# First-layer weights moved in three whole transfers behind the first unit's product, and the second chunk's loads released by units 1 and 2

## The chip, the cores and the metric

The kernel runs on one core of one Trainium2 chip. The metric is the device time of one execution in microseconds (us); the time of the kernel before is 248.93 us, the median of three runs that lie between 248.78 and 249.1 us. One more execution was recorded by the hardware profiler, and every row below is from it.

## The reference, cut to what matters

A linear attention with a decaying state is followed by a two-layer feed-forward network with SiLU. The attention runs over batch 4, 8 heads, 768 steps and 48 channels a head; the network has 3072 tokens of 384 values and a hidden width of 2048.

```python
def _attn_ref(r, k, v, w, u):
    state = np.zeros((B, H, D, D), dtype=np.float32)
    for t in range(S):
        kt, vt, rt = (k[:, :, t].copy(), v[:, :, t].copy(), r[:, :, t].copy())
        cur = np.einsum('bhd,bhe->bhde', u[None] * kt, vt)
        y[:, :, t] = np.einsum('bhd,bhde->bhe', rt, state + cur)
        state = w[None, :, :, None] * state + np.einsum('bhd,bhe->bhde', kt, vt)

def _moe_ref(x, w_in, w_out):
    h = x @ w_in
    g = h * (1.0 / (1.0 + np.exp(-h)))
    return g @ w_out
```

All inputs and the output are float32. The attention's output, as 3072 rows of 384, is the network's x.

## The kernel before

The 768 steps are cut into 6 chunks of 128. A **unit** is one chunk of one batch element: 24 units, unit i being chunk i // 4 of batch i % 4. Units 0 to 3 are the first chunk, and from unit 4 on a unit also needs the state that the unit four before it left.

Inputs live in four slots (`rin`, `kin`, `vin`, NIN = 4), so unit 4 loads into the slot of unit 0. `load(i)` (line 63) issues three transfers from SyncE, for r, k and v of a unit. Each brings 192 KB, in pieces of 48 values (192 bytes). Units 0 to 3 are loaded at the start. SyncE's queue is in program order, so a transfer that has to wait holds all that stand behind it.

For each unit there are four steps, spread over four turns of the main loop (line 303), s being the turn:

- `p1(s)` transposes r and k of unit s on TensorE (`tr`, `tk`, line 172), and VectorE scales them out of PSUM (`rT`, `kT`). In the same turn `natural(s)` puts on GpSimd the three products `ku`, `rku_f` and `kc` (lines 148, 150, 151) and casts v on ScalarE (line 146). `bonus(s)` reduces `rku_f` on VectorE and makes `vu` from it on GpSimd (line 160).
- `p2(s - 1)` makes the scores of the unit before (`ae`, `ao`, lines 186 and 188) and masks them (`am`).
- `p3(s - 2)` makes the outputs `y` and the state's update `sps` (lines 208 and 216).
- `p4(s - 3)` transposes the output into `xT` (lines 254, 255), the network's input.

The network's work is cut into pieces that the list `fillers` holds; `fill(2)` puts some of it between the attention's steps. A block of units adds its pieces once its last unit is through `p4`. The first block is units 0 and 1, so its first-layer matmuls (`hps`, line 263) come behind `p1(4)`, `p2(3)`, `p3(2)` and `p4(1)` in TensorE's order. They read `win` (three tiles of 128 x 2048 in float16, one for each 128 of the 384 inputs), and the second layer's (`ops`, line 275) read `wout`.

Both weights are float32 in memory and are cast to float16 by the transfer itself, which GpSimd issues: `win` in twelve transfers of 128 x 512 in turn 1 (line 310), `wout` in four of 128 x 4 x 384 in turn 3 (line 315). GpSimd takes its instructions in order too, so its products for the units stand behind the issues.

The loads of units 4, 5 and 6 are issued in turn 3. The first of them is made to wait, by a dependency written by hand, for `last_pool[3]`, the `vu` of unit 3, which stands behind the issues of `wout` on GpSimd. From turn 4 on `load(s + 3)` follows turn by turn. The four state tiles `st` are cleared by GpSimd in turn 0 (line 321).

Of the kernel before, what the change touches and what calls it, by code (L numbers as in the profile page):

```python
# [11 lines left out]
ALU = mybir.AluOpType  # L12
# [3 lines left out]
def kernel(  # L16
# [11 lines left out]
    nc = tc.nc  # L28

    B, H, S, D = r.shape  # L30
# [8 lines left out]
    NQ = HD // 128  # L39
    NU = B * NCH  # L40
    NIN = 4
    NKC = 3
# [9 lines left out]
    kin = [big.tile([128, H, 64], FP, name=f"kin{i}") for i in range(NIN)]  # L52
    vin = [big.tile([128, H, D], FP, name=f"vin{i}") for i in range(NIN)]
    kc = [big.tile([128, H, 64], F16, name=f"kc{i}") for i in range(NKC)]
    st = [big.tile([PR, NP, PW], FP, name=f"st{b}") for b in range(B)]
    st16 = [big.tile([PR, NP, PW], F16, name=f"stb{b}") for b in range(B)]
    win = [big.tile([128, DFF], F16, name=f"win{q}") for q in range(NQ)]
    wout = big.tile([128, NFT, HD], F16)

    def unit(i):  # L60
        return divmod(i, B)

    def load(i, after=None):
        if i >= NU:
            return
        sc, b = unit(i)
        for t, src in ((rin, r), (kin, k), (vin, v)):
            d = nc.sync.dma_start(out=t[i % NIN][:, :, 0:D],
                                  in_=src[b, :, sc * C:sc * C + C, :]
                                  .rearrange("h t d -> t h d"))  # L70
            if after is not None:
                tc.add_manual_dep(d.ins, after.ins.name,
                                  mybir.DependencyInfo(mybir.DependencyClass.Sync,
                                                       mybir.DependencyReason.DATA),
                                  reason="the weights go first")
                after = None
# [4 lines left out]
    for p0, o in ((0, 0), (64, D)):  # L81
        nc.scalar.dma_start(out=wpT[p0:p0 + D, :],
                            in_=bass.AP(tensor=w.tensor, offset=o, ap=[[1, D], [PW, NP]]))
# [9 lines left out]
    for t in (rin, kin):  # L93
# [7 lines left out]
        out=maskM, in_=maskM, compare_op=ALU.is_ge, fill=0.0,  # L101
# [19 lines left out]
    n = 1  # L121
    while n < C:
        for t, o in ((pw, 1), (iw, 0)):
            nc.vector.tensor_tensor(
                out=t[:, :, o + n:o + 2 * n], in0=t[:, :, o:o + n],
                in1=t[:, :, o + n - 1:o + n].broadcast_to([PR, NP, n]), op=ALU.mult)
# [6 lines left out]
    lamC = cst.tile([128, H, D], FP)  # L133
# [5 lines left out]
    last_pool = {}  # L139

    def natural(i):

        n = i % NIN
        L = live.setdefault(i, {})
        L["v16"] = wrk.tile([128, H, D], F16, name="v16", bufs=4)
        nc.scalar.copy(out=L["v16"], in_=vin[n])
        ku = wrk.tile([128, H, D], FP, name="ku")
        nc.gpsimd.tensor_tensor(out=ku, in0=kin[n][:, :, 0:D], in1=u_bc, op=ALU.mult)  # L148
        L["rku_f"] = wrk.tile([128, H, D], FP, name="rku_f")
        nc.gpsimd.tensor_tensor(out=L["rku_f"], in0=rin[n][:, :, 0:D], in1=ku, op=ALU.mult)  # L150
        nc.gpsimd.tensor_tensor(out=kc[i % NKC][:, :, 0:D], in0=kin[n][:, :, 0:D],  # L151
                                in1=lamC, op=ALU.mult)

    def bonus(i):
        L = live[i]
        rku = wrk.tile([128, H], FP, name="rku")
        nc.vector.tensor_reduce(out=rku, in_=L["rku_f"], axis=mybir.AxisListType.X,  # L157
                                op=ALU.add)
        L["vu"] = wrk.tile([128, H, D], FP, name="vu", bufs=3)
        last_pool[i] = nc.gpsimd.tensor_tensor(  # L160
            out=L["vu"], in0=vin[i % NIN],
            in1=rku.unsqueeze(2).broadcast_to([128, H, D]), op=ALU.mult)

    def p1(i):
        n = i % NIN
        L = live.setdefault(i, {})
        tr = ps.tile([128, NP, C], FP, name="tr", tag="ps", bufs=8)
        tk = ps.tile([128, NP, C], FP, name="tk", tag="ps", bufs=8)
        for t, src in ((tr, rin), (tk, kin)):
            flat = src[n].rearrange("p h d -> p (h d)")  # L170
            for p in range(NP):
                nc.tensor.transpose(t[0:PR, p, :], flat[:, 128 * p:128 * p + PR], ident)  # L172
        L["rT"] = wrk.tile([PR, NP, C], FP, name="rT")
        nc.vector.tensor_tensor(out=L["rT"], in0=tr[0:PR], in1=lamR, op=ALU.mult)  # L174
        L["kT"] = wrk.tile([PR, NP, C], FP, name="kT")
        nc.vector.tensor_tensor(out=L["kT"], in0=tk[0:PR], in1=lamK, op=ALU.mult)  # L176
        if i >= B:
            L["rT16"] = wrk.tile([PR, NP, C], F16, name="rT16", bufs=3)
            nc.scalar.copy(out=L["rT16"], in_=L["rT"])  # L179

    def p2(i):
        L = live[i]
        ae = ps.tile([128, NP, C], FP, name="ae", tag="ps", bufs=8)
        ao = ps.tile([128, NP, C], FP, name="ao", tag="ps", bufs=8)
        for p in range(NP):
            nc.tensor.matmul(ae[:, p, :], L["kT"][0:D, p, :], L["rT"][0:D, p, :],  # L186
                             start=True, stop=True)
            nc.tensor.matmul(ao[:, p, :], L["kT"][64:PR, p, :], L["rT"][64:PR, p, :],  # L188
                             start=True, stop=True)
        L["am"] = []  # L190
        for a in (ae, ao):
            am = wrk.tile([128, NP, C], F16, name="am", bufs=4)
            nc.vector.tensor_tensor(out=am, in0=a,  # L193
                                    in1=maskM.unsqueeze(1).broadcast_to([128, NP, C]),
                                    op=ALU.mult)
            L["am"].append(am)
# [49 lines left out]
    def p4(i):  # L246
        L = live.pop(i)
        bl = block_of[i]
        if bl.xT is None:
            bl.xT = wrk.tile([128, NQ, B, C], F16, name="xT", bufs=3)  # L250
        yT = ps.tile([128, NQ, C], F16, name="yT", tag="ps", bufs=8)
        yf = L["y16"].rearrange("p h d -> p (h d)")
        for q in range(NQ):
            nc.tensor.transpose(yT[:, q, :], yf[:, 128 * q:128 * q + 128], ident16)  # L254
        nc.scalar.copy(out=bl.xT[:, :, bl.units.index(i), :], in_=yT)  # L255
# [28 lines left out]
    def moe(bl):  # L284
        w1 = bl.n / B
        for ft in range(NFT):
            yield w1, lambda ft=ft: l1(bl, ft)
        for j in range(bl.n):
            for part in range(4):
                yield 1.0, lambda j=j, part=part: l2(bl, j, part)  # L290
# [4 lines left out]
    def fill(n):  # L295
        owed[0] = min(owed[0] + n, n + 1.0)
        while fillers and owed[0] > 0:
            w_, f = fillers.pop(0)
            owed[0] -= w_
            f()  # L300


    for s in range(NU + 3):
        if s < NU:
            p1(s)
            natural(s)
        if s == 1:
            for g in range(4):
                for q in range(NQ):
                    nc.gpsimd.dma_start(out=win[q][:, 512 * g:512 * g + 512],  # L310
                                        in_=moe_w_in[128 * q:128 * q + 128,
                                                     512 * g:512 * g + 512])
        if s == 3:
            for g in range(4):
                nc.gpsimd.dma_start(
                    out=wout[:, 4 * g:4 * g + 4, :],
                    in_=moe_w_out[512 * g:512 * g + 512, :]
                    .rearrange("(f p) n -> p f n", p=128))
        if s == 0:
            for b in range(B):  # L320
                nc.gpsimd.memset(st[b], 0.0)
        fill(2)
        if 0 <= s - 1 < NU:
            p2(s - 1)
        fill(2)
        if s < NU:
            bonus(s)
        if s == 3:
            load(4, after=last_pool[3])
            load(5)  # L330
            load(6)
        elif s > 3:
            load(s + 3)
        if 0 <= s - 2 < NU:
            p3(s - 2)
        fill(2)
        if 0 <= s - 3 < NU:
            p4(s - 3)
            bl = block_of[s - 3]
            if s - 3 == bl.units[-1]:  # L340
                fillers.extend(moe(bl))
        fill(2)
# [31 lines left out]
```

## Time and profile before

| what | value |
|---|---|
| median of three runs | 248.93 us |
| profiled execution | 249.69 us |
| its span, first to last instruction | 248.0 us |
| TensorE busy | 204.4 us, 82% |
| GpSimd busy | 125.7 us, 51% |
| mean granted clock of TensorE | 0.924 of 2.4 GHz |
| moved by the queue of SyncE (q1) | 18.88 MB |
| moved by the queue of GpSimd (q0) | 3.15 MB, counted as written |

In the part of the page with 40 slices of the span, each slice is 6.2 us and each digit a busy share in tenths. The chain of waits is followed back from the last instruction: each row is a piece of work, or a transfer, that the next one had to wait for. In a timeline the bracket behind a row tells how long the engine had stood idle and what ended it. In a table by windows each row is one stretch, with the busy time of each engine and, last, TensorE's granted clock, the busy share of the 16 DMA engines (it goes above 1, as packets overlap) and the rate at which bytes were written.

### The profile page before, as it was taken

The numbers are of one execution on the slowest core, as the hardware profiler recorded it, in microseconds if no ns is written. First come the engines' busy times: TensorE is split into PE (matmuls) and PEld (weight loads), VectorE is DVE, ScalarE is ACT, GpSimd is POOL, SyncE is SP. The second block draws the span as 40 slices with busy tenths as digits, with TensorE's granted clock in tenths as the row PEclk, the third lists the DMA queues.
The fourth block names the chain that finished last, engine by engine and source line by source line (L and its number), as shares of the span: only waits on it lengthen the run. The fifth ranks groups of instructions, "written<-read, shape, count | busy, mean of one in ns | idle before, by whom it ended". The sixth has DMA issues, their size and how long they took to land.

```text
span 248.0 us, 4555 instructions
## 1 busy us (share of the span) xinstructions
PE 204.4 (82%) x1720; PEld 137.6 (56%) x1720; DVE 117.3 (47%) x233; ACT 94.9 (38%) x185; POOL 125.7 (51%) x166
## 2 busy tenths in 40 slices
PE   2691000599999994999999999999999999999994
PEld 2480000468678781666675667655667565654462
DVE  3960450246465676545674556565547552230011
ACT  2510000156347133574216661237731267217700
POOL 3696991462564688685567456764676620000000
PEclk9998555559999998899999999999999999999999
DMA  7999639999174379530747903479101100010011
GB/s 144 181 138 133 106 45 195 187 171 137 33 135 90 89 140 151 102 66 3 127 115 140 129 3 80 107 138 162 30 27 39 63 3 0 32 66 33 0 63 63
DMA packets 82901, 22.70 MB, mean 92 GB/s; under 512 B 75968, under 2 KB 82880, under 8 KB 82880
## 3 DMA queue, kind: packets, MB, share of 16 engines
q1 hardware_dynamic: 78336, 18.88, 45.2%
q0 software_dynamic: 3840, 3.15, 8.8%
q10 hardware_dynamic: 704, 0.40, 0.8%
q8 instruction: 13, 0.21, 0.4%
q14 instruction: 8, 0.07, 0.1%
HBM read 20.84 MB, written 4.72 MB: 103 GB/s over the span
## 4 chain that ended last, share of the span: by engine, by line
PE 72%; POOL 12%; DMA 9%; issue 3%; ACT 2%; DVE 1%; SPq 0%; POOLq 0%; DVEq 0%
PE hps L263 27%; PE ops L275 24%; PE ae L186 8%; DMA kin<-in_k_dram 4%; PE tr L172 4%; DMA rin<-in_r_dram 3%; PE tk L172 3%; POOL rku_f L150 2%; POOL ku L148 2%; POOL kc L151 2%; DMA win<-in_moe_w_in_dram 2%; POOL vu L160 2%; PE y L208 2%; PE yT L254 1%; PE sps L216 1%
## 5 line engine op out<-in xcount | busy, mean ns | idle before, releaser
L263 PE MATMUL hps<-xT,win 128*128 128x512 f16 (+1 forms) x336 | 72.0, 361 | 7.0 <-ACT xT L255 7.0
L275 PE MATMUL ops<-wout,gT 128*128 128x384 f16 x384 | 69.3, 326 | 0.0
L266 ACT ACTIVATE gT<-hps 128x512 f16<-128x512 f32 (+1 forms) x112 | 57.8, 536 | 22.3 <-PE hps L263 20.6
L263 PEld LDWEIGHTS <-win 128*128 128x128 f16 x336 | 32.5, 101 | 32.3 <-issue 7.3
L275 PEld LDWEIGHTS <-gT 128*128 128x128 f16 x384 | 36.0, 98 | 21.7
L160 POOL TENSOR_TENSOR vu<-vin,rku 128x384 f32<-128x384 f32 x24 | 19.9, 830 | 44.7 <-DVE rku L157 44.7
L172 PE MATMUL tr<-ident,rin 128*112 128x128 f32 x96 | 17.2, 310 | 22.6 <-DMA rin<-in_r_dram 20.2
L255 ACT COPY xT<-yT 128x384 f16<-128x384 f16 x24 | 11.5, 477 | 58.1 <-PE yT L254 58.1
L174 DVE TENSOR_TENSOR rT<-tr,pw 112x512 f32<-112x512 f32 x24 | 16.6, 690 | 34.9 <-PE tr L172 34.8
L148 POOL TENSOR_TENSOR ku<-kin,u_bc 128x384 f32<-128x384 f32 x24 | 24.1, 1004 | 12.5 <-DMA kin<-in_k_dram 9.2
L179 ACT CAST rT<-rT 112x512 f16<-112x512 f32 x20 | 12.4, 618 | 46.8 <-DVE rT L174 46.8
L186 PE MATMUL ae<-rT,kT 48*128 48x128 f32 x192 | 29.9, 300 | 0.0
L188 PE MATMUL ao<-rT,kT 48*128 48x128 f32 x192 | 29.8, 299 | 0.0
L193 DVE TENSOR_TENSOR am<-ae,maskM 128x512 f16<-128x512 f32 x24 | 16.6, 690 | 28.0 <-PE ao L188 28.0
L186 PEld LDWEIGHTS ae<-rT,kT 48*128 48x128 f32 x192 | 25.1, 200 | 7.9 <-DVE kT L176 3.5
L172 PEld LDWEIGHTS tr<-ident,rin 128*112 128x112 f32 x96 | 12.9, 152 | 25.9 <-issue 21.1
L279 DVE COPY osb<-ops 128x384 f32<-128x384 f32 x24 | 13.3, 554 | 26.9 <-PE ops L275 26.5
L150 POOL TENSOR_TENSOR rku_f<-rin,ku 128x384 f32<-128x384 f32 x24 | 24.1, 1005 | 1.9
L151 POOL TENSOR_TENSOR kc<-kin,lamC 128x384 f16<-128x384 f32 x24 | 24.1, 1002 | 2.0 <-ACT lamC L134 2.0
L188 PEld LDWEIGHTS ao<-rT,kT 48*128 48x128 f32 x192 | 25.0, 200 | 0.0
L229 DVE TENSOR_TENSOR st<-sps,sdec 48x192 f32<-48x192 f32 x32 | 11.4, 355 | 18.9 <-POOL sdec L223 13.0
L157 DVE TENSOR_REDUCE rku<-rku_f 128x8 f32<-128x384 f32 x24 | 13.1, 545 | 11.3 <-POOL rku_f L150 11.2
(46 smaller groups left out, 205.2 us busy)
## 6 DMA issues: line engine op xcount, KB each, us to landing
rin<-in_r_dram SPq DMA_DIRECT2D x24, 192.0 KB, 4.4
kin<-in_k_dram SPq DMA_DIRECT2D x24, 192.0 KB, 4.5
vin<-in_v_dram SPq DMA_DIRECT2D x24, 192.0 KB, 4.6
out_dram<-osb SPq DMA_DIRECT2D x24, 192.0 KB, 1.9
win<-in_moe_w_in_dram POOLq DMA_DIRECT2D x12, 128.0 KB, 6.6
wout<-in_moe_w_out_dram POOLq DMA_DIRECT2D x4, 384.0 KB, 6.7
u_bc<-in_u_dram ACTq DMA_DIRECT2D x1, 192.0 KB, 4.0
w_bc<-in_w_dram ACTq DMA_DIRECT2D x1, 192.0 KB, 5.0
```

The source lines that it names most:

```text
L148: nc.gpsimd.tensor_tensor(out=ku, in0=kin[n][:, :, 0:D], in1=u_bc, op=ALU.mult)
L150: nc.gpsimd.tensor_tensor(out=L["rku_f"], in0=rin[n][:, :, 0:D], in1=ku, op=ALU.mult)
L151: nc.gpsimd.tensor_tensor(out=kc[i % NKC][:, :, 0:D], in0=kin[n][:, :, 0:D], in1=lamC, op=ALU.mult)
L160: last_pool[i] = nc.gpsimd.tensor_tensor(out=L["vu"], in0=vin[i % NIN], in1=rku.unsqueeze(2).broadcast_to([128, H, D]), op=ALU.mult)
L172: nc.tensor.transpose(t[0:PR, p, :], flat[:, 128 * p:128 * p + PR], ident)
L174: nc.vector.tensor_tensor(out=L["rT"], in0=tr[0:PR], in1=lamR, op=ALU.mult)
L186: nc.tensor.matmul(ae[:, p, :], L["kT"][0:D, p, :], L["rT"][0:D, p, :], start=True, stop=True)
L188: nc.tensor.matmul(ao[:, p, :], L["kT"][64:PR, p, :], L["rT"][64:PR, p, :], start=True, stop=True)
L193: nc.vector.tensor_tensor(out=am, in0=a, in1=maskM.unsqueeze(1).broadcast_to([128, NP, C]), op=ALU.mult)
L263: nc.tensor.matmul(hps[:, 0:n], win[q][:, ft * 128:(ft + 1) * 128], bl.xT[:, q, 0:bl.n, :].rearrange("p b t -> p (b t)"), start=(q == 0), ...
L266: nc.scalar.activation(out=bl.gT[:, ft, 0:n], in_=hps[:, 0:n], func=AF.Silu)
L275: nc.tensor.matmul(ops, bl.gT[:, ft, j * C:(j + 1) * C], wout[:, ft, :], start=(ft == 0), stop=(ft == NFT - 1))
```

## The change

GpSimd issues the first-layer weights as three transfers of 128 x 2048, inside `natural(0)`, between `rku_f` and `kc` of unit 0. `wout` is issued in turn 2 and not in turn 3. `last_pool` now names `kc` of a unit and not its `vu`. `load(4)` is issued in turn 1 and tied to `kc` of unit 1, `load(5)` in turn 2 and tied to `kc` of unit 2, and `load(6)` in turn 3, untied. The four clears of `st` go to VectorE and into turn 1.

```diff
@@ natural
+        if i == 0:
+            for q in range(NQ):
+                nc.gpsimd.dma_start(out=win[q], in_=moe_w_in[128 * q:128 * q + 128, :])
+        last_pool[i] = nc.gpsimd.tensor_tensor(
+            out=kc[i % NKC][:, :, 0:D], in0=kin[n][:, :, 0:D], in1=lamC, op=ALU.mult)
@@ bonus
-        last_pool[i] = nc.gpsimd.tensor_tensor(
+        nc.gpsimd.tensor_tensor(
             out=L["vu"], in0=vin[i % NIN],
@@ the main loop
-        if s == 1:
-            for g in range(4):
-                for q in range(NQ):
-                    nc.gpsimd.dma_start(out=win[q][:, 512 * g:512 * g + 512],
-                                        in_=moe_w_in[128 * q:128 * q + 128,
-                                                     512 * g:512 * g + 512])
-        if s == 3:
+        if s == 2:
             for g in range(4):
                 nc.gpsimd.dma_start(
                     out=wout[:, 4 * g:4 * g + 4, :],
...
-        if s == 0:
+        if s == 1:
             for b in range(B):
-                nc.gpsimd.memset(st[b], 0.0)
+                nc.vector.memset(st[b], 0.0)
...
-        if s == 3:
-            load(4, after=last_pool[3])
-            load(5)
-            load(6)
-        elif s > 3:
+        if s == 1:
+            load(4, after=last_pool[1])
+        elif s == 2:
+            load(5, after=last_pool[2])
+        elif s > 2:
             load(s + 3)
```

On TensorE and ScalarE the order of the instructions is the same in both kernels, and on SyncE's queue too. On GpSimd, this stands around the issue of `win` in the kernel before (kin_74 and vin_78 are of unit 1, kin_75 of unit 2, kc_82 is unit 1's product; the dots leave out the nine other transfers of `win`):

```order
L150 TENSOR_TENSOR rku_f<-rin_70,ku 128x384
L151 TENSOR_TENSOR kc_82<-kin_74,lamC 128x8x48
L310 DMA win_92<-in_moe_w_in_dram 128x512
L310 DMA win_93<-in_moe_w_in_dram 128x512
L310 DMA win_94<-in_moe_w_in_dram 128x512
...
L160 TENSOR_TENSOR vu<-vin_78,rku 128x384
L148 TENSOR_TENSOR ku<-kin_75,u_bc 128x384
```

In the changed kernel it stands in unit 0 (kin_73 and vin_77), still on GpSimd:

```order
L150 TENSOR_TENSOR rku_f<-rin_69,ku 128x384
L153 DMA win_92<-in_moe_w_in_dram 128x2048
L153 DMA win_93<-in_moe_w_in_dram 128x2048
L153 DMA win_94<-in_moe_w_in_dram 128x2048
L154 TENSOR_TENSOR kc_81<-kin_73,lamC 128x8x48
L163 TENSOR_TENSOR vu<-vin_77,rku 128x384
L148 TENSOR_TENSOR ku<-kin_74,u_bc 128x384
```

So the issue of `win` has moved ahead of `kc` and `vu` of unit 0 and of all products of unit 1, and nine issues are gone.

Around the issue of `wout` GpSimd has this before (kin_76, rin_72 and vin_80 are of unit 3, vin_79 is of unit 2):

```order
L160 TENSOR_TENSOR vu<-vin_79,rku 128x384
L233 CAST stb_88<-st_84 112x384
L148 TENSOR_TENSOR ku<-kin_76,u_bc 128x384
L150 TENSOR_TENSOR rku_f<-rin_72,ku 128x384
L151 TENSOR_TENSOR kc_81<-kin_76,lamC 128x8x48
L315 DMA wout<-in_moe_w_out_dram 128x4x384 x4
L160 TENSOR_TENSOR vu<-vin_80,rku 128x384
```

And this in the changed kernel:

```order
L148 TENSOR_TENSOR ku<-kin_75,u_bc 128x384
L150 TENSOR_TENSOR rku_f<-rin_71,ku 128x384
L154 TENSOR_TENSOR kc_83<-kin_75,lamC 128x8x48
L312 DMA wout<-in_moe_w_out_dram 128x4x384 x4
L163 TENSOR_TENSOR vu<-vin_79,rku 128x384
L236 CAST stb_88<-st_84 112x384
L148 TENSOR_TENSOR ku<-kin_76,u_bc 128x384
```

The four issues of `wout` have moved one unit forward, behind `kc` of unit 2, so that `vu` of unit 2 and everything of unit 3 now come after them.

## Rows read from the trace of the kernel before

**Rows 1.** The page's 40 slices of the span: tenths busy, clock, DMA

```profile
PE   2691000599999994999999999999999999999994
PEclk9998555559999998899999999999999999999999
DMA  7999639999174379530747903479101100010011
```

**Rows 2.** The chain of waits: start us, length us, what

```profile
33.51 3.05 POOL wout L315 x4
...
37.44 8.33 DMA rin<-in_r_dram
...
47.08 1.08 PE tk L172 x4
...
51.90 4.00 PE hps L263 x18
...
70.81 2.13 PE hps L263 x18
```

**Rows 3.** Timeline of GpSimd: start us, us, line, operation, tiles

```profile
7.14 1.04 POOL L150 TENSOR_TENSOR rku_f<-rin,ku 128x384 f32<-128x384 f32 x1
...
10.17 1.00 POOL L151 TENSOR_TENSOR kc<-kin,lamC 128x384 f16<-128x384 f32 x1 [1.98 <-ACT lamC L134]
11.11 1.49 POOL L321 MEMSET st<- 112x384 f32 x4
...
16.32 5.51 POOL L310 DMA_DIRECT2D win<-in_moe_w_in_dram  x10
...
26.26 0.99 POOL L148 TENSOR_TENSOR ku<-kin,u_bc 128x384 f32<-128x384 f32 x1
...
28.29 0.99 POOL L151 TENSOR_TENSOR kc<-kin,lamC 128x384 f16<-128x384 f32 x1
...
47.01 1.00 POOL L148 TENSOR_TENSOR ku<-kin,u_bc 128x384 f32<-128x384 f32 x1 [9.16 <-DMA kin<-in_k_dram]
```

**Rows 4.** Timeline of ScalarE: the casts of v of units 2 and 3

```profile
14.49 0.51 ACT L146 CAST v<-vin 128x384 f16<-128x384 f32 x1 [2.95 <-DMA vin<-in_v_dram]
17.62 0.51 ACT L146 CAST v<-vin 128x384 f16<-128x384 f32 x1 [2.62 <-DMA vin<-in_v_dram]
```

**Rows 5.** Windows of 1 us; last are clock, DMA share, GB/s

```profile
17.00:18.00 1.00, 1.00 (x12) 0.82 (x12) 1.00 (x3) 0.38 (x1) 1.00 (x3) 1.00 0.20 20
18.00:19.00 1.00, 1.00 (x23) 0.88 (x22) 0.41 (x1) 0.13 (x1) 1.00 (x3) 1.00 1.05 151
...
20.00:21.00 1.00, 0.00 (x0) 0.00 (x0) 0.00 (x0) 0.00 (x0) 1.00 (x3) 1.00 0.77 75
21.00:22.00 1.00, 0.00 (x0) 0.00 (x0) 0.00 (x0) 0.00 (x0) 0.83 (x2) 1.00 1.04 110
...
25.00:26.00 1.00, 0.00 (x0) 0.00 (x0) 0.00 (x0) 0.00 (x0) 0.98 (x2) 0.50 1.23 202
...
35.00:36.00 1.00, 0.00 (x0) 0.00 (x0) 0.00 (x0) 0.00 (x0) 1.00 (x3) 0.50 0.78 48
36.00:37.00 1.00, 0.00 (x0) 0.00 (x0) 0.00 (x0) 0.00 (x0) 1.00 (x2) 0.50 1.13 174
```

**Rows 6.** What the DMA engines moved from 8 to 16 us

```profile
DMA packets 7185, 1.36 MB, mean 170 GB/s; under 512 B 7185, under 2 KB 7185, under 8 KB 7185
```

**Rows 7.** The same from 16.3 to 28.3 us, then from 23 to 28 us

```profile
DMA packets 2119, 1.64 MB, mean 137 GB/s; under 512 B 610, under 2 KB 2118, under 8 KB 2118
...
DMA packets 972, 0.89 MB, mean 178 GB/s; under 512 B 105, under 2 KB 972, under 8 KB 972
```

**Rows 8.** Packets by queue: from 39 to 42 us, then 45 to 46 us

```profile
q0 software_dynamic: 767, 0.57, 122.7%
q1 hardware_dynamic: 128, 0.02, 7.2%
...
q1 hardware_dynamic: 1227, 0.23, 135.9%
```

More of the change, by code (lines that the diff above doesn't have):

```diff
@@ L150, in natural @@
         nc.gpsimd.tensor_tensor(out=L["rku_f"], in0=rin[n][:, :, 0:D], in1=ku, op=ALU.mult)
-        nc.gpsimd.tensor_tensor(out=kc[i % NKC][:, :, 0:D], in0=kin[n][:, :, 0:D],
-                                in1=lamC, op=ALU.mult)
+        if i == 0:
[3 more added lines that the diff above has]
+            out=kc[i % NKC][:, :, 0:D], in0=kin[n][:, :, 0:D], in1=lamC, op=ALU.mult)
     def bonus(i):
```

## The prediction

> **What bounds the kernel now.** I read the slices first. From unit 5 or so on TensorE is busy at nine tenths nearly everywhere, and the change touches nothing there. What is idle is the start: the fifth to seventh slice, from 24.8 to 43.4 us, hold a TensorE that does nothing, at a clock fallen to half, and a DMA share that falls to 3 between two full stretches [rows 1]. So the question is what unit 4 waits for, since the network's first matmuls stand behind it on TensorE.
>
> The chain of waits answers it: the issue of `wout` to 36.56, then the load of unit 4's r, issued at 37.44 and 8.33 us on its way, then the transposes of unit 4, with `tk` at 47.08, and the first `hps` at 51.90 [rows 2]. GpSimd got its first operand of unit 4, k, at 47.01, after 9.16 us of idling [rows 3]. Behind 51.90 one piece of TensorE's work follows the other. So the time until k of unit 4 (kin4) has landed is the term that the change can move, and all behind it should move with it.
>
> Why does kin4 land at 46.9 only? By then the DMA engines have had to bring four things: the twelve loads of units 0 to 3, the last of them landed at 17.6 [rows 4]; `win`, about 18 to 28 us [rows 5, 7]; `wout`, from 35 to just under 45 [rows 5, 8]; and rin4 and kin4. Between `win` and `wout`, from 28.3 to 35.0, there is next to nothing: GpSimd does the products of units 2 and 3 first, since they stood behind the issues of `win`. Beside `wout` the loads hardly move: from 39 to 42 us the queue of GpSimd (q0) got 767 packets and the loads' queue (q1) 128, and kin4 needed the 1.9 us from 45.0, when q0 is gone, to 46.9 [rows 3, 8].
>
> **The change part by part.** The sum is made against the profiled execution, whose span is 248.0 us and whose time is 249.69, 0.76 above the median of the runs; a shift in the span is taken off the median as it is.
>
> *Issue of `win`.* `rku_f` of unit 0 ends at 8.18, and GpSimd then idles 1.98 us until `lamC` is there for `kc` at 10.17 [rows 3]. Three issues in the old form take 3 x 5.51/10 = 1.65 us and fit there. No row shows an issue of 128 x 2048; between 0.55 us each (the rows are 128 as before) and four times that, 2.2, `kc` of unit 0 is late by 0 to 4.6 us. I take 0.55, by the number of rows, but it hardly matters: GpSimd will then wait for k of unit 2 until about 22, and its products of units 0 and 1 are six of about 1 us and two `vu`. The nine issues less on GpSimd are covered by the same wait.
>
> *`win`'s transfer.* First data came 1.7 us after the first issue (16.32 to 18.0) [rows 3, 5], so now 9.9. It is 3 x 128 x 2048 x 2 bytes = 1.57 MB as written. Its rate was 137 GB/s over the whole stretch, with starting and issuing in it, and 178 once GpSimd had issued nearly all [rows 7]; the ends are 137 and the best second, 202 [rows 5], thus 11.5 and 7.8 us. I take 178, since all three are issued when data starts: 8.8 us, to 18.7. Meanwhile the loads of units 1 to 3 that have not landed are pushed back by just this, as `wout` pushed unit 4's: vin of unit 3 from 17.6 to 26.4. Loads came 1.04 us apart ((17.62 - 14.49)/3) [rows 4], so k of unit 2 landed at 13.4 and now at 22.2.
>
> *`wout`.* GpSimd needs 3.02 us from there to the end of `kc` of unit 2 (26.26 to 29.28 for the three) [rows 3]: issue at 25.2. The first issue was at 33.51, and full rate came at 36.0, 2.5 us later, after a second of 48 GB/s [rows 2, 5]: now 27.7. From 26.4 to 27.7 the loads have the engines to themselves, as load(4) was released by `kc` of unit 1 long before; 1.3 us at 170 GB/s [rows 6] is 0.22 MB, one load of 0.197 and little more. So r of unit 4 gets through, k does not. `wout`, 1.52 MB after its slow second, moved at 1.5 MB in the 8.9 us from 36.0 to 44.9, loads beside it: 36.6. Then k's rest. It took 1.9 us from `wout`'s end before; with nearly all of r gone ahead I keep 0.7 to 1.9, and take 0.9: 37.5.
>
> *Sum.* kin4 at 37.5 and not 46.9, **9.4 us earlier**. Next late after it would be GpSimd: issues of `wout` 25.2 to 28.3, then `vu`, `stb` and unit 3's four products, some 6 us, to about 34.5. It is in time, with 3 us to spare.
>
> *The rest at nothing.* `vu` of units 1 and 2 comes behind fewer issues or the same. The four clears of `st` leave GpSimd (1.49 us [rows 3], under the same wait) and go to VectorE. No row has them there; between nothing and GpSimd's 1.49 us, `am` of unit 0 is late by that, while VectorE is idle from 20 to 22 and at 25 us [rows 5]. load(5) and load(6) follow load(4) on SyncE in the same order, and unit 5 is wanted 8 us after unit 4, as before. Twelve transfers made three save nothing of themselves: they were in flight together.
>
> *Two clocks.* TensorE's granted clock is at half from about 25 to 56 us, and for a while again near 100 [rows 1], and what it costs is seen in the 18 `hps`: 4.00 us cold, 2.13 at full clock [rows 2]. Unit 4's work comes after an idle stretch in either kernel, so I take no difference; an earlier or later rise is worth up to 1.9 us either way.
>
> **A rule that speaks against it.** Rows 8 show six packets of the weights to one of the loads. The Trainium skill ("DMA: Bandwidth & Descriptors", section "Issuing engines are not separate DMA queues") says that transfers issued by different engines run on the same 16 DMA engines and interleave. By that, issuing `win` earlier gains no bandwidth, and the trace agrees as far as it goes: the sum above moves `win` into time taken from the loads. What it leaves as gain is only the idle time between 28.3 and 35.0 (6.7 us) and the slow seconds at 20 to 22 and 35, with which the sum's 9.4 agrees.
>
> **The rivals.**
>
> *Even turns.* The two queues could share the engines evenly when both have work waiting, which the trace of before shows only for loads that start late beside `wout`. Then from 9.9 on the loads run at half rate: 7.7 us of them left, and 2.3 for r and k of unit 4, make 10.0, at half rate 20.0, so kin4 lands at 29.9, 17 us earlier; `win` has then landed too, and GpSimd, with k of unit 3 at 23, is done by 28 or so. Time 248.93 - 17.0 = 231.9. Much the same follows if `wout` starts 1.5 us later than I work out, since kin4 is then through before it. Against it: 767 to 128. The Trainium skill (same page, section "Queues, rings and completion order") says that an engine goes round robin over its queue rows, a packet at a time; by that a queue with small packets gets little, and the trace has 6 to 1 by packets and more by bytes.
>
> *Whole rows are slow, a little.* Rows of 2048 could move at what the engines did while `win` was being issued, 110 GB/s at 21 us [rows 5]: 14.3 us, not 8.8. The gain shrinks to 3.9: 245.0.
>
> *Whole rows are slow, much: slower than before.* The place is the same, `win` from 9.9 on, with the loads of units 2 to 4 behind it. kin4 is no earlier than before when `win` takes 8.8 + 9.4 = 18.2 us, that is 86 GB/s. One second of the trace stands under this, with 75 [rows 5]. At 75, 21.0 us, kin4 lands at 49.7, and the time is 251.7. For it: no such transfer is in the trace. Against it: 75 was one second, early, amid issues, and longer rows mean fewer packets for the same bytes.
>
> *The tie does nothing.* load(4) stands in SyncE's queue behind the loads of unit 3, and those end at 26.4 here. So tying it to unit 1 instead of unit 3 has no worth of its own beyond the 0.2 MB before `wout`; without these r would come after `wout` too, at a cost of about 1 us. That lies in the forecast's spread.
>
> **How the numbers follow.** Forecast, with weights ahead of loads: 0.76, time 248.93 - 9.4 = 239.5. Even turns or k ahead of `wout`: 0.12, 231.9. Little gain: 0.08, 245.0. Slower: 0.04, 251.7. The forecast's spread: `win` 7.8 to 11.5 us (+1.0, -2.7), k's rest 0.7 to 1.9 (+0.2, -1.0), the clock 1.9 each way. All at once would be 233.9 and more than 245; I take 235.8 to 243.3, which holds nearly all of the forecast's 0.76 and the edges of its neighbours. About 0.2% (0.5 us) is what a measurement of this kernel can tell from no change; faster by more 0.95, within 0.01, slower by more 0.04.
>
> **What the profile after would show.** Right, step by step: q0 moves from 10 to about 19 us and q1 nearly stops there; ScalarE's cast of v of unit 3 at about 26; `wout`'s issue near 25; DMA share without a gap from 2 to 45 us; `tr` of unit 4 well before `tk`, and `tk` near 37.5; first `hps` near 42.5; from there on the same distances as before. Wrong: q1 running on through `win` (even turns); q0 still busy with `win` after 21 (slow rows); a GpSimd that is still at unit 3 when k of unit 4 is there; or a first `hps` at 42 whose gain is given back by 100 us, which would make a wait behind unit 4 the bound.

## The result, and the profile after

The changed kernel takes **232.94 us** (median of four runs, 232.68 to 235.77) against 248.86 us for the kernel before (four runs, 248.53 to 249.1). The ratio is 0.939, with a 95% interval from 0.931 to 0.946: 15.9 us less, where 9.4 were forecast. The time lies below the forecast's range (235.8 to 243.3) and about 1 us above the rival "even turns or k ahead of `wout`" (231.9). The profiled execution took 233.19 us, its span is 231.5 us (before 248.0), and the mean granted clock rose from 0.924 to 0.977.

The page's slices of the kernel after, 5.8 us each, show where it went, beside [rows 1]:

```profile
PE   2544957999999399999999999999999999999993
PEclk9999988999999769999999999999999999999999
DMA  7999999976347955016686044792011000120011
```

TensorE is at nine tenths from the eighth slice on, but for the fourteenth, that is from about 40 us and not from 50. Of the long stretch at half clock at the start two slices at 8 are left (in windows of 2 us the granted clock is 0.83 from 32 us, 0.50 from 34 and 0.82 from 36, and 1.00 on both sides). The DMA engines are full from the second slice to the eighth with no valley between. The chain of waits (start us, length us, what), beside [rows 2]:

```profile
8.36 12.04 DMA kin<-in_k_dram
20.45 1.10 PE tk L175 x4
...
25.72 13.36 DMA kin<-in_k_dram
79.47 4.00 PE hps L266 x9
```

Neither the issue of `wout` nor the load of unit 4 is in it any more. The two loads in it are k of unit 2 (8.36 to 20.4, pushed back by `win`) and k of unit 5 (25.72 to 39.1, issued and then held beside `wout`). GpSimd's timeline (start us, us, line, operation, tiles), beside [rows 3]:

```profile
8.22 1.82 POOL L153 DMA_DIRECT2D win<-in_moe_w_in_dram  x3
10.03 1.03 POOL L154 TENSOR_TENSOR kc<-kin,lamC 128x384 f16<-128x384 f32 x1
...
20.47 1.00 POOL L148 TENSOR_TENSOR ku<-kin,u_bc 128x384 f32<-128x384 f32 x1 [3.92 <-DMA kin<-in_k_dram]
...
23.44 3.05 POOL L312 DMA_DIRECT2D wout<-in_moe_w_out_dram  x4
...
28.83 1.01 POOL L150 TENSOR_TENSOR rku_f<-rin,ku 128x384 f32<-128x384 f32 x1
...
39.16 1.01 POOL L148 TENSOR_TENSOR ku<-kin,u_bc 128x384 f32<-128x384 f32 x1 [2.78 <-DMA kin<-in_k_dram]
```

The three issues of `win` take 0.61 us each and fit into the time in which GpSimd waited for `lamC`, as worked out. Unit 4's `ku` comes at 32.05 without a wait, after 9.16 us of waiting before [rows 3]. The wait that is left is unit 5's, 2.78 us at 39.16. TensorE's timeline shows the same (in brackets the idle time ahead, and what ended it):

```profile
27.94 0.60 PE L175 MATMUL tr<-ident,rin 128*112 128x128 f32 x4
28.67 0.65 PE L175 MATMUL tk<-ident,kin 128*112 128x128 f32 x4
...
33.80 3.54 PE L266 MATMUL hps<-xT,win 128*128 128x256 f16 x18 [2.51 <-ACT xT L258]
38.41 0.62 PE L175 MATMUL tr<-ident,rin 128*112 128x128 f32 x4 [1.08 <-DMA rin<-in_r_dram]
39.22 0.62 PE L175 MATMUL tk<-ident,kin 128*112 128x128 f32 x4 [0.19 <-DMA kin<-in_k_dram]
...
79.47 4.00 PE L266 MATMUL hps<-xT,win 128*128 128x512 f16 x9 [3.65 <-ACT xT L258]
```

The first `hps` starts at 33.80 and not at 51.90: 18.1 us earlier, forecast 42.5. It waits for `xT`, which stands behind unit 4's `rT` on ScalarE, and that chain goes back to GpSimd's `rku_f` of unit 3 (ended 29.84). VectorE's timeline shows the link:

```profile
29.87 0.55 DVE L160 TENSOR_REDUCE rku<-rku_f 128x8 f32<-128x384 f32 x1 [0.93 <-POOL rku_f L150]
...
31.55 0.69 DVE L177 TENSOR_TENSOR rT<-tr,pw 112x512 f32<-112x512 f32 x1
```

Then unit 5's `tk` is at 39.22, where it was at 56.53 before (17.3 us earlier), and nine `hps` at half clock (4.00 us at 79.47; the granted clock is 0.50 from 79 to 83) were 3.33 us at 96.75 before, which takes back 0.7. That gives 16.6, and the span is 16.5 us shorter. So the gain is made before 34 us, and 1.6 us of it are lost again to unit 5's loads and to the clock.

### The profile page after: what moved, and what is told of

Its sections match the earlier page's. It is cut to its first block, busy times and chain, and to the rows that moved or that the text cites. A ratio compares the mean times of both kernels' runs of the same rounds, so it can differ in the third digit from the quotient of the medians.

```text
span 231.5 us, 4545 instructions
## 1 busy us (share of the span) xinstructions
PE 204.3 (88%) x1720; PEld 136.9 (59%) x1720; DVE 118.7 (51%) x237; ACT 94.8 (41%) x185; POOL 119.6 (52%) x153
## 4 chain that ended last, share of the span: by engine, by line
PE 77%; DMA 12%; POOL 3%; SPq 2%; ACT 2%; DVE 1%; issue 1%; DVEq 0%; POOLq 0%
PE hps L266 28%; PE ops L278 26%; DMA kin<-in_k_dram 11%; PE ae L189 9%; PE tk L175 4%; PE tr L175 4%; PE y L211 2%; SPq L68 2%; PE sps L219 2%; DMA rin<-in_r_dram 1%; PE yT L257 1%; PE y L208 1%; ACT xT L258 1%; POOL vu L163 1%; POOL sdec L226 1%
## 5 line engine op out<-in xcount | busy, mean ns | idle before, releaser
L163 POOL TENSOR_TENSOR vu<-vin,rku 128x384 f32<-128x384 f32 x24 | 20.0, 832 | 41.5 <-DVE rku L160 41.5
L196 DVE TENSOR_TENSOR am<-ae,maskM 128x512 f16<-128x512 f32 x24 | 16.5, 687 | 27.4 <-PE ao L191 27.4
L189 PE MATMUL ae<-rT,kT 48*128 48x128 f32 x192 | 29.9, 299 | 0.0
L177 DVE TENSOR_TENSOR rT<-tr,pw 112x512 f32<-112x512 f32 x24 | 16.6, 690 | 22.4 <-PE tr L175 22.3
L175 PE MATMUL tk<-ident,kin 128*112 128x128 f32 x96 | 16.6, 301 | 6.7 <-DMA kin<-in_k_dram 6.3
L179 DVE TENSOR_TENSOR kT<-tk,iw 112x512 f32<-112x512 f32 x24 | 16.3, 681 | 5.5 <-PE tk L175 5.3
```

The source lines that it names most:

```text
L163: nc.gpsimd.tensor_tensor(out=L["vu"], in0=vin[i % NIN], in1=rku.unsqueeze(2).broadcast_to([128, H, D]), op=ALU.mult)
L196: nc.vector.tensor_tensor(out=am, in0=a, in1=maskM.unsqueeze(1).broadcast_to([128, NP, C]), op=ALU.mult)
```

## How the loads and the weights share the engines

Two windows of the DMA view decide the case. In the kernel after, the packets by queue (packets, MB, share of 16 engines) from 12 to 18 us and, of that, from 13 to 18; then from 24 to 25, 25 to 26 and 26 to 27 us; and from 30 to 36 us:

```profile
q0 software_dynamic: 329, 1.22, 100.1%
q1 hardware_dynamic: 255, 0.05, 7.0%
...
q0 software_dynamic: 279, 1.01, 99.9%
q1 hardware_dynamic: 255, 0.05, 8.4%
...
q1 hardware_dynamic: 899, 0.17, 145.2%
...
q1 hardware_dynamic: 710, 0.13, 122.5%
q0 software_dynamic: 29, 0.02, 18.7%
...
q0 software_dynamic: 198, 0.15, 104.5%
q1 hardware_dynamic: 131, 0.02, 20.9%
...
q0 software_dynamic: 1159, 0.87, 92.1%
q1 hardware_dynamic: 1162, 0.22, 33.8%
```

From 12 to 18 us `win` moves at 1.22 MB in 6 us (203 GB/s), and the loads get 255 packets, where 899 is what they get in one microsecond alone. All 255 come after 13 us; from there to 18 `win` has 279. From 30 to 36 us the loads get 1162 beside `wout`, as many packets as `wout` has. Once both queues move they have about the same number of packets, and what differs is the packet: 192 bytes of a load against some 3,700 of `win` and 750 of `wout`. The prediction had read six to one from [rows 8]. The same stretch of the kernel before, cut anew from 37.5 to 41 us and from 41.5 to 44 us:

```profile
q0 software_dynamic: 944, 0.70, 131.1%
...
q0 software_dynamic: 490, 0.36, 92.8%
q1 hardware_dynamic: 489, 0.09, 33.7%
```

The first cut has no row of q1: the loads, issued from 37.44 on, hadn't begun by 41. The second is one to one. Rows 8 averaged a second of sharing with two in which the loads weren't there. The Trainium skill ("DMA: Bandwidth & Descriptors", section "Queues, rings and completion order") says that an engine goes round robin over the queue rows with work, a packet at a time; 1159 to 1162 agrees with that, and 767 to 128 never spoke against it. By the same section of the Trainium skill a packet typically holds about 9 to 17 descriptors. The packets of the profile are single rows, and no count here shows turns of that size.

## The experiments

Twelve runs, of the changed kernel and nine variants, were made in three sets of four; those of a set ran on one chip and share the runs of the kernel before (medians 249.82, 249.87 and 249.56 us). In these sets GpSimd's first `ku` comes at 6.6 to 7.6 us and not at 6.15 as in the profile above, so moments are compared within a set, or by what waits for what, and times by their ratio to the kernel before. All compute the whole output. The changed kernel itself is in the second and third set.

**Theory A**: the gain comes from r and k of unit 4 getting through ahead of `wout`, which takes both the tie and a gap between the loads and the weights. The rivals are that the tie does nothing, and that the place or the form of the transfers of `win` is what brings the gain.

### Set 1: the tie taken out, the tie alone

`e1_tie_late` is the changed kernel with the second chunk's loads released as before, by `vu` of unit 3:

```diff
-        if s == 1:
-            load(4, after=last_pool[1])
-        elif s == 2:
-            load(5, after=last_pool[2])
-        elif s > 2:
+        if s == 3:
+            load(4, after=last_vu[3])
+            load(5)
+            load(6)
+        elif s > 3:
             load(s + 3)
```

> The changed kernel with only the release of the loads put back: load(4) is tied to vu of unit 3 and issued in turn 3 with load(5) and load(6). In the changed kernel that vu ended at 31.6 us. Theory A (the early release is the larger part of the gain, because the loads' queue is then already full when the second-layer weights start): r of unit 4 is issued at 31.7, lands at about 35.5, k at about 36.5, first-layer matmuls of the network start near 41.4 and not 33.8, time 240.5 us. Rival (as I predicted: the release has no worth of its own, since the loads stand behind the weights anyway): no more than 1 us lost, 233 to 234 us.

Measured: 241.4 us (240.55 to 241.82), ratio 0.966 [0.961, 0.970]. TensorE's timeline:

```profile
37.42 1.07 PE L176 MATMUL tr<-ident,rin 128*112 128x128 f32 x4 [7.98 <-DMA rin<-in_r_dram]
...
43.41 4.00 PE L267 MATMUL hps<-xT,win 128*128 128x256 f16 x18 [0.57 <-ACT xT L259]
```

That is theory A's figure and not the rival's. The load of r of unit 4 is issued at 33.09, TensorE waits 7.98 us for it, and its work is cold again (18 `hps` in 4.00 us). From its issue to its landing r took 4.2 us, no more than the median of all such loads in the kernel after (4.6): `wout` was nearly through by then (48 packets of it are left after 35 us, against 1144 of the loads from 35 to 36). So what is lost here is the 12 us by which the issue comes later (21.16 in the kernel after), not a load that is slow beside `wout`. The time and the moments are close to what the prediction had worked out, `hps` at 42.5 and 239.5 us, while the change itself is 9 us from it at `hps`. In both, k of unit 4 comes behind `wout`.

`e4_tie_only` is the kernel before with nothing but the release of the loads changed (`last_pool` names `kc`, and the block of loads is that of the change). `win` stays in twelve transfers in turn 1, `wout` in turn 3, the clears on GpSimd.

> The kernel before with only the release of the loads changed: load(4) behind kc of unit 1, load(5) behind kc of unit 2, load(6) in turn 3; first-layer weights still in twelve transfers in turn 1. Theory A: k of unit 4 lands by about 25 beside the first-layer weights; then GpSimd's chain bounds (rku_f of unit 3 ends at 32.6 as before), the first-layer matmuls start near 36.5 to 37 and not 51.9: 233 to 234 us, nearly all of the gain by this part alone. Rival (the gain comes from moving the first-layer weights; the release does nothing): 248 to 249 us.

Measured: 235.78 us (234.77 to 236.58), ratio 0.943 [0.938, 0.949]. TensorE's and, under it, GpSimd's timeline:

```profile
37.66 4.00 PE L263 MATMUL hps<-xT,win 128*128 128x256 f16 x18 [1.29 <-ACT xT L255]
```

```profile
34.66 3.05 POOL L315 DMA_DIRECT2D wout<-in_moe_w_out_dram  x4
```

And the loads of r and k of unit 4 in the DMA view of 17 to 18 us (last, us from issue to landing):

```profile
rin<-in_r_dram SPq DMA_DIRECT2D x1, 192.0 KB, 3.5
kin<-in_k_dram SPq DMA_DIRECT2D x1, 192.0 KB, 6.3
```

The tie alone brings 14.0 us, a little less than theory A had (233 to 234 us). Issued at 17.25 and 17.71, r and k of unit 4 land at 20.8 and 24.0, beside `win`, as theory A had it ("by about 25"). The time between `win` and `wout` that stood empty before goes to unit 5's loads, issued from 30.45. So for unit 4 the gap that theory A asks for beside the tie isn't needed: it is enough that its loads are through before `wout`. Set side by side as ratios to the kernel before:

| | loads released late | loads released by units 1 and 2 |
|---|---|---|
| `win` in turn 1, `wout` in turn 3 | 1 | 0.943 (e4) |
| `win` in turn 0, whole, `wout` in turn 2 | 0.966 (e1) | 0.939, 0.940, 0.939 (the change: the result, sets 2 and 3) |

Each part shortens the same wait, so their gains (14.0 us for the tie, 8.4 for the rest) don't add up. With the tie in place, the rest of the change is worth 0.3 to 0.4% (on other chips), within the intervals.

### Set 1 and 2: where `win` is issued

`e8_win_turn1` is the changed kernel with the three whole transfers issued in turn 1, behind `kc` of unit 1, and `wout` in turn 2 as in the change:

```diff
-        if i == 0:
-            for q in range(NQ):
-                nc.gpsimd.dma_start(out=win[q], in_=moe_w_in[128 * q:128 * q + 128, :])
...
+        if s == 1:
+            for q in range(NQ):
+                nc.gpsimd.dma_start(out=win[q], in_=moe_w_in[128 * q:128 * q + 128, :])
```

> The changed kernel with the three whole transfers of the first-layer weights issued in turn 1, behind kc of unit 1, and not in unit 0's products. The loads of units 0 to 3 are then nearly through when the weights move (from about 17 us), but r and k of unit 4 stand beside them and beside the second-layer weights, which follow at once. Theory A (one packet for one): about 60 packets of the loads per us beside rows of 4096 bytes, 192 beside rows of 768; k of unit 4 at about 33, first-layer matmuls near 38, 237.5 us. Rival (weights first, the loads nearly still until both weights are through): k of unit 4 at 35 or later, matmuls at 40, 239.5 us.

Measured: 236.96 us (235.19 to 238.41), ratio 0.948 [0.941, 0.954]. TensorE, and the packets from 28 to 36 us:

```profile
34.40 1.07 PE L172 MATMUL tk<-ident,kin 128*112 128x128 f32 x4 [4.16 <-DMA kin<-in_k_dram]
```

```profile
q0 software_dynamic: 1576, 1.17, 93.5%
q1 hardware_dynamic: 1579, 0.30, 33.9%
```

Here `wout` was issued at 21.29, with `win` still on its way; there is no gap, r and k of unit 4 share both weights one packet for one, and TensorE waits 7.33 us for r and 4.16 for k. By the medians that is 0.9% behind the change, with intervals that overlap a little. The time is near theory A's figure; the first `hps`, at 39.76, lies nearer the rival's 40, though in this set all moments are over a microsecond later. What settles it is the count: 1576 to 1579, where the rival has the loads nearly still.

`e6_win_turn2` puts `win` one turn later still, behind `kc` of unit 2, and `wout` into turn 3:

```diff
-        if s == 1:
+        if s == 2:
             for q in range(NQ):
                 nc.gpsimd.dma_start(out=win[q], in_=moe_w_in[128 * q:128 * q + 128, :])
-        if s == 2:
+        if s == 3:
```

> The changed kernel with each weight one step later: the first layer's three whole transfers in turn 2 behind kc of unit 2, the second layer's in turn 3 behind kc of unit 3; loads released as in the changed kernel. Theory A (the engines serve one packet of each queue in turn, so what is ahead of the weights in the loads' queue is through before them, and what is behind them is held): k of unit 2 at 14 and of unit 4 at about 21 us, first-layer weights from 21 to 29, first-layer matmuls from about 30 and not 33.8; r and k of unit 5 then stand beside the second-layer weights until about 37.5, against 39.1: 2.5 us faster than the changed kernel, 230.5 us. Rival (GpSimd's issues, 3 us for the second layer's, set the pace wherever they stand): first matmuls not before 33, same time as the changed kernel, 233 us.

Measured: 233.3 us (232.31 to 234.12), ratio 0.933 [0.930, 0.937]; the change beside it in this set, 235.57, ratio 0.940 [0.936, 0.944]. TensorE:

```profile
31.92 3.38 PE L263 MATMUL hps<-xT,win 128*128 128x256 f16 x16 [2.12 <-DMA win<-in_moe_w_in_dram]
...
36.70 0.62 PE L172 MATMUL tk<-ident,kin 128*112 128x128 f32 x4 [0.96 <-DMA kin<-in_k_dram]
```

`win` itself is now waited for, 2.12 us; and yet the kernel is 2.3 us faster than the change by the medians, with intervals that just touch. The absolute time is the rival's (233), but the change beside it is slower on this chip too, and the difference is theory A's (2.5 us faster, against none). So is the start: two of the first `hps` run at 29.22 and the others from 31.92, where theory A has 30 and the rival nothing before 33. GpSimd no longer waits for k of unit 2, as it did for 5.18 us in the change beside it.

`a2_after_again` is the change itself on the chip of this set; its time is above.

> The changed kernel itself, run again on the same chip as the next three, so that they are compared with it directly: 233 us, ratio to the kernel before 0.93 to 0.94.

Its profile has k of unit 5 at 41.2 and the same two waits, for r and k of unit 5, as in the profile after.

### Where `wout` is issued

`e2_wout_turn3` (set 1) is the changed kernel with `wout` one turn later (`if s == 3:`).

> The changed kernel with only the second-layer weights put back into turn 3, behind kc of unit 3. Theory A (what bounds the start of the changed kernel is GpSimd's chain through the issue of these weights, 3.05 us, and then r and k of unit 5, which move beside them one packet for one): the issue comes at about 28.5, units 4 and 5 land before the weights move (k of unit 5 at about 31 and not 39.1), the first-layer matmuls start near 31.7 and not 33.8 and unit 5 is not waited for: 229.5 to 230.5 us, unless the second layer then waits for its weights (up to 2 us of it back). Rival (the gap at the start is set by the loads of unit 4 alone, landed at 28.6 either way): no change, 232.9 us.

Measured: 232.92 us (232.7 to 233.77), ratio 0.933 [0.928, 0.939]: no clear difference from the change (0.939 to 0.940 in the other sets), as the rival had it and not theory A. TensorE, then VectorE:

```profile
39.51 0.65 PE L175 MATMUL tk<-ident,kin 128*112 128x128 f32 x4 [1.93 <-DVE y L222]
```

```profile
38.43 0.55 DVE L160 TENSOR_REDUCE rku<-rku_f 128x8 f32<-128x384 f32 x1 [3.12 <-POOL rku_f L150]
```

The rival's reason doesn't hold, though. Unit 5's loads are no longer waited for, as theory A had it, but unit 4's products stand behind the 3.06 us of issues on GpSimd, VectorE waits 3.12 us for `rku_f`, and `tk` of unit 5 comes at 39.51. In the two profiles of the change in which GpSimd starts as late as here (a2, a3) it comes at 41.34 and 40.69. A new wait on TensorE (1.93 us) took the place of the old ones (3.10 us in a2, 0.86 in a3); by the medians 0.6% is left, within the intervals.

`e7_win2_wout4` (set 2) is `e6` with `wout` in turn 4, behind unit 4's products:

> As the kernel with the first-layer weights in turn 2, but with the second layer's in turn 4, behind kc of unit 4. Theory A: first-layer matmuls from about 30 us, unit 5 landed by 31 and not waited for, second-layer weights from 32 to 42, just in time for the second layer: 5 to 6 us faster than the changed kernel, 227 to 228.5 us. Rival (the second layer then waits for its weights, or GpSimd's products of units 4 and 5 come late): the gain is given back, 231 to 234 us.

Measured: 230.05 us (229.31 to 231.76), ratio 0.921 [0.918, 0.925]. `tk` of unit 5 waits for nothing here. By the medians it is 5.5 us faster than the change beside it, as theory A had it (5 to 6), though the weights are waited for, as the rival had it; the time lies between the two figures. It stands a second time, in the third set, as `e11_win2_wout4_again`, with the change beside it as `a3_after_third`.

> The version with the first-layer weights in turn 2 and the second layer's in turn 4 once more, beside the changed kernel on one chip: 5 us faster than it, 229 to 231 us.

> The changed kernel a third time, so that the next three are compared with it on one chip: 233 to 236 us.

Measured: e11 230.47 us (229.52 to 231.18), ratio 0.923 [0.920, 0.927]; the change 233.86 us (233.07 to 236.25), ratio 0.939 [0.934, 0.944]. TensorE of e11:

```profile
28.79 0.58 PE L263 MATMUL hps<-xT,win 128*128 128x256 f16 x2 [2.45 <-ACT xT L255]
31.30 3.20 PE L263 MATMUL hps<-xT,win 128*128 128x256 f16 x16 [1.93 <-DMA win<-in_moe_w_in_dram]
...
44.49 1.46 PE L275 MATMUL ops<-wout,gT 128*128 128x384 f16 x8 [1.22 <-DMA wout<-in_moe_w_out_dram]
```

Each weight is late by one to two microseconds, and the loads are not waited for on TensorE. So the weights here come after the loads and nearly in time, where the change has them early and the loads late. This version is faster than both kernels: by 19.8 and 19.1 us than the one before, and by 5.5 and 3.4 than the change, in the two sets (5 were expected of the second).

### The form of the transfers, and the clears

`e3_quarters` (set 2) is the changed kernel with `win` in the old twelve transfers of 128 x 512, at the new early place:

```diff
-            for q in range(NQ):
-                nc.gpsimd.dma_start(out=win[q], in_=moe_w_in[128 * q:128 * q + 128, :])
+            for g in range(4):
+                for q in range(NQ):
+                    nc.gpsimd.dma_start(out=win[q][:, 512 * g:512 * g + 512],
+                                        in_=moe_w_in[128 * q:128 * q + 128,
+                                                     512 * g:512 * g + 512])
```

> The changed kernel with the first-layer weights in twelve transfers of 128 x 512 at the same early place. Theory A (whole transfers matter only through GpSimd, which issues three and is free, while twelve hold it until the first ones have landed): GpSimd's kc of unit 0 near 17 to 18 us and not 11, kc of unit 2 some 2 us later than in the changed kernel, 1 to 2 us slower: 234 to 235 us; loads beside the weights get one packet for one of 1024 bytes. Rival (long rows are what makes the weights fast): the weights take 11.5 us and not 8, 3 to 4 us slower: 236 to 237 us.

Measured: 235.14 us (234.16 to 236.97), ratio 0.942 [0.937, 0.946], the same as the change on that chip (235.57), neither theory A's 1 to 2 us slower nor the rival's 3 to 4. But the way there is another. GpSimd's timeline, and the packets from 16 to 20 us:

```profile
9.85 4.46 POOL L154 DMA_DIRECT2D win<-in_moe_w_in_dram  x8
...
19.60 1.01 POOL L157 TENSOR_TENSOR kc<-kin,lamC 128x384 f16<-128x384 f32 x1
```

```profile
q0 software_dynamic: 621, 0.57, 92.6%
q1 hardware_dynamic: 646, 0.12, 25.1%
```

Again one packet for one, now with rows of 1024 bytes: the loads get 162 packets a microsecond (646/4) beside 51 (255/5) next to whole rows. `win` moves at 143 GB/s in these 4 us and not at 203, GpSimd is held until 19.6 by issues that wait for landings, `wout` goes out at 28.10, and the first `hps` comes at 38.38; on the other side unit 5's loads are not waited for. Two effects of the form are shown and they cancel here; that the whole rows bring a gain is not.

`e9_halves_turn2` (set 3) is `e7` with `win` in six transfers of 128 x 1024, all the first halves ahead of the second, so that the first `hps` needn't wait for all of `win`:

> That version with the first-layer weights in six transfers of 128 x 1024, the first half of the columns of all three first. There the first-layer matmuls stopped after two of them, from 29.9 to 32.3 us, until the last whole transfer had landed. Theory A (whole transfers hold back the first columns): the matmuls start near 29 and run on, 2 to 3 us faster: 227 to 228.5 us. Rival (the second layer's weights, moving from 32 to 43 us, are the next to be waited for): less than 1 us faster, 229 to 230 us.

Measured: 231.69 us (230.51 to 232.47), ratio 0.928 [0.924, 0.932], beside 0.923 of e11: no better, and by the medians 1.2 us worse, though the intervals overlap. Both figures were too low, theory A's (227 to 228.5) and the rival's (229 to 230). TensorE:

```profile
30.42 3.76 PE L263 MATMUL hps<-xT,win 128*128 128x256 f16 x18 [2.29 <-ACT xT L255]
...
43.82 1.25 PE L275 MATMUL ops<-wout,gT 128*128 128x384 f16 x4 [2.17 <-DMA wout<-in_moe_w_out_dram]
```

The wait for `win` is gone, but six issues take 3.40 us of GpSimd and not 1.81, `wout` goes out at 31.71 and not at 30.07, and the wait is now there, 2.17 us, as the rival had it.

`e10_clears_back` (set 3) is the changed kernel with the clears of `st` on GpSimd in turn 0 again.

> The changed kernel with the four clears of st back on GpSimd and in turn 0. Theory A (GpSimd waits some 4 us for k of unit 2 behind them, so they cost nothing): the same time within 0.5 us. Rival (GpSimd's chain is the bound, so 1.5 us on it are 1.5 us of the time): 1.5 us slower.

Measured: 234.08 us (233.2 to 236.58), ratio 0.939 [0.935, 0.943], the same as the change beside it, as theory A had it. On VectorE the four clears take 1.60 us in the changed kernel's trace, and the time does not tell the two places apart.

## Why the prediction was wrong in size, by its steps

**The bound was read rightly.** Unit 4's loads set the time, and when they came earlier, all behind moved with them: 18.1 us at the first `hps`, 16.5 at the end.

**Held.** The issue of `win` at 8.2 in GpSimd's free time; the clears at nothing (e10); `hps` some 5 us behind k of unit 4 where k is the bound (e1: k at 38.5, `hps` at 43.41). Rows of 2048 were not slow, so both slow rivals fell.

**"It moved at 178 GB/s"** was too little: whole rows went at 203 GB/s from 12 to 18 us, close to the range's best end, 202. k of unit 2 was there at 20.4 and not at 22.2, and `wout` issued at 23.44 and not at 25.2.

**"1.3 us, one load: r gets through, k does not"** is the step that failed. I let the loads of unit 4 begin when v of unit 3 had landed. In the kernel before, 12477 of some 12480 packets of the first twelve loads and the constants on their queue were through by 17.0, while v of unit 3 was cast only at 17.62 [rows 4]; in the kernel after it is the same:

```profile
q1 hardware_dynamic: 12462, 2.36, 72.2%
```

That is until 23.6 us, and v of unit 3 is cast at 24.97. So the engines took up the next load 0.6 to 1.4 us before the last one's cast could start. `wout` took hold at 26.0, by the windows above, and not at 27.7. The gap is therefore 2.4 us and not 1.3, enough for both loads (1024 packets each, at 899 a microsecond 2.3 us). The faster `win` moved both of its ends; what made it longer is its start, which I took from a landing: from the cast at 24.97 to 26.0 it would be 1.0. The DMA view of `kin`'s issue at 22.28 and of the one at 25.72:

```profile
DMA to landing us min/median/max: 4.8/4.8/4.8
...
DMA to landing us min/median/max: 13.4/13.4/13.4
```

k of unit 4 landed at 27.1, forecast 37.5; k of unit 5, which missed the gap, took 13.4. The rival had named this branch ("k is then through before it"), and I gave it, with its other form, 0.12, although only 1.5 us, by my own words, in a chain of estimates each off by as much, stood between it and the forecast. That the time came out so near its 231.9 is in part luck: the branch had no sum of its own, and the 231.9 was worked out for even shares beside `win`, with k of unit 4 at 29.9 and all of the 17 us kept.

**"Six to one"** was misread, as shown above: the share is one packet for one, as from 41.5 to 44 us of the kernel before. For the forecast's own path this changed nothing, since it had k wait for `wout`'s end in any case; but it was the ground on which I held the rival low. Its other form, half of the bytes for the loads beside `win`, didn't come either: they got 4% of them there (0.05 of 1.27 MB), as their packets are that small.

**"The tie does nothing"** fell clearest: e1 without it gives back 6.3 to 6.7 us of 15.9 (by the ratios), and e4 with it alone has 14.0. The argument was that load(4) stands behind unit 3's loads anyhow. It does: its tie, `kc` of unit 1, was met at 15.1, but SyncE's issues of r and k of unit 3 took 6.27 and 3.04 us, from 10.61 to 20.0, and r of unit 4 went out at 21.16. But the tie decides whether it goes out before `wout` begins or only when `wout` is nearly through (33.09 in e1).

**"Next late would be GpSimd, with 3 us to spare"**: with k at 27.1 GpSimd is indeed the bound, through `rku_f` of unit 3 at 29.84, so `hps` comes 6.7 us behind k of unit 4 and not 5. A GpSimd still at unit 3 when k of unit 4 is there was one of the signs of being wrong that I had named. **"Unit 5 is wanted 8 us after unit 4, as before"**: it was wanted earlier than its loads could come past `wout`, and that wait (1.08 and 0.19 us on TensorE, 2.78 on GpSimd) is a new one.

**The clock.** I took no difference. The granted clock is no longer at half long before the first `hps`, but it falls as they start (0.50 from 34 to 36 us), and the 18 of them take 3.54 us. In other profiles of the same kernel they take 2.13 us (a2) or 4.00 (a3); in a2 the clock falls later instead, during the waits for unit 5 (0.53 from 40 to 42, 0.50 from 42 to 46). This is within the 1.9 us either way that was allowed; it may be part of the spread of the change's runs, 232.7 to 237.2 over its three sets of runs, but what decides it in one run wasn't settled.

**The range.** Its fast end was summed wrongly: 1.0, 0.2 and 1.9 off 239.5 make 236.4, not 233.9, for which the losses were taken as gains. The range as stated was wide enough on that side by its own terms; the measured time lies below it because a term was mis-sized by more than its bounds.

## What to carry to other kernels

Where weights and small-row loads share the DMA engines, the order in which they are handed over decides: what has moved before the bulk transfer's packets begin comes at full rate, and what is still waiting then gets a packet for a packet, which with rows of 192 bytes is little: k of unit 5, issued 0.3 us before `wout` took hold, took 13.4 us. So look first at what releases a load, then at where the bulk transfer is issued; and let the bulk come just in time behind the loads, not early in front of them (e7 and e11 were the fastest versions here). Count a gap between transfers from the last packet, not from the start of what waits for it, and when a row of packet counts carries an argument, cut the window until both queues are active throughout it.

## What was not expected of the hardware

- Two busy queues share by packets, not by bytes: 1159 to 1162 in 6 us (rows of 768 bytes beside 192), 621 to 646 in 4 us (1024 beside 192), 279 to 255 in 5 us (4096 beside 192).
- In the kernel before, loads issued from 37.44 on, with weights busy, had no packet until 41. In e1, loads issued from 33.09 had 16 packets by 35, when `wout` was all but through. With the engines nearly free, loads issued from 30.45 on in e4 had 368 by 32. In the kernel after, the loads' queue had 66 packets from 11 to 12 us, as `win` took hold, and none from 12 to 13; and in e4, from 39 to 41 us, loads on their way got 147 beside 489 of `wout`, before the counts were even again (202 to 201 from 42 to 43). So the even share holds once both queues are in step; why it takes so long to get there was not tried and stays open.
- Weights in whole rows moved faster than in quarters: 203 GB/s as written (12 to 18 us) against 143 in e3 (16 to 20 us), issued at the same place, loads beside them in both.
